# Where VectorE's share of the low parts stands, and which buffer holds their h: a fused attention and maxout kernel

## The chip, the core and the metric

One core of a Trainium2 chip. TensorE multiplies matrices (in the profile PE, with PEld for its weight loads), VectorE (DVE), ScalarE (ACT) and GpSimd (POOL) work on elements, SyncE's queue (SP) starts DMAs. SBUF is the working memory, PSUM holds eight banks of 128 x 512 f32 that TensorE writes. The metric is the time on the device in microseconds (us) of one execution. Before the change it is 818.93 us, the median of three runs from 818.26 to 819.09.

## The reference

```python
def _attn_ref(x, inducing):                    # x: (4, 12544, 128), inducing: (32, 128)
    def mab(q, kv):
        s = scale * (q @ kv.transpose(0, 2, 1))
        s = s - s.max(-1, keepdims=True)
        a = np.exp(s)
        a /= a.sum(-1, keepdims=True) + 1e-09
        return a @ kv
    h = mab(I, x)
    return mab(x, h).astype(np.float32)

def _moe_ref(x, w1, w2, w3, w_out):            # w1, w2, w3: (128, 768), w_out: (768, 128)
    h = np.maximum(np.maximum(x @ w1, x @ w2), x @ w3)
    return (h @ w_out).astype(np.float32)
```

The output of the first goes through the second, all in f32.

## The kernel before, in words

For each of the four batches, a first phase pools all tokens into 32 states h (softmax over tokens), and a second phase computes, for every token, softmax weights over those 32 states and from them the maxout and the last product. The first phase of batch 0 runs alone at the start; from then on the second phase of one batch runs with the first phase of the next beside it.

**The second phase's pipeline.** The 98 tiles of 128 tokens of a batch are one short group of 2 tiles and six full groups of 16. A full group is four chunks of 512 columns, and each chunk has six slots, one for each 128 of the 768 hidden units. So a full group is a window of 24 slots, numbered 0 to 23 here, and is called by (batch, group). For each slot:

- TensorE multiplies the weights `pT` with two sets of columns into the banks `pu` (line 819) and `pv` (825), which alternate between two banks each;
- ScalarE takes the relu of `pu` (834), VectorE the maximum of that and `pv` (852): this is `h`, 128 x 512;
- ScalarE rounds `h` to fp32r, the high part `hi` (841), and one engine subtracts that from `h`, the low part `lo`: GpSimd (849) for most slots, VectorE (855) for a few;
- six slots later TensorE adds wo_hi x hi, wo_lo x hi and wo_hi x lo to the chunk's output bank `acc` (898). At the first of a chunk's slots a product of its own (894) starts that bank afresh.

There are two output banks (`bank_o`). While one collects a chunk, the other holds the chunk before until it is copied out (`finish`, 910), and is idle after that until the next chunk's line 894; `spare[0]` names it.

**What sets the order.** `main` writes the instructions of all engines slot by slot, by hand, and each engine runs its own in that order. `advance` writes a slot: a subtraction that VectorE is to do is kept in `pipe["low"]` and written one step after GpSimd's would be, behind the maximum of the slot two on. Beside the slots, `plan` puts other work at chosen slots of a window:

- `softmax2`: the weights of the next group, VectorE and ScalarE steps at slots 3 to 15 (742 to 776);
- `turn`: the first phase of the next batch, 18 turns in all, one a window from (0,1) to (2,4). TensorE writes scores at slot 2, which holds up the slots' products for about 3 us; VectorE reduces them at slot 4 (407); GpSimd swaps the maxima between partition halves and quarters by small copies L429 at slots 5 and 9 (`turn_swap`; a copy L419 at slot 4 adds the last maximum); VectorE reduces the swapped ones by L437 at slots 8 (`mq`) and 11 (`mm`). Windows (0,1) and (0,2) have a second turn 12 slots later, whose last products come at slot 14 of the window after;
- in group 5 the next batch's states are put together (`invert_total`, `combine_states`, `combine_low`).

**Which slots are VectorE's.** `Chunk.low` says for which slots VectorE subtracts; `in_bank` says whether the `h` of such a slot is written to the second `aux` bank (`bank_a[1]`) or to one of five SBUF buffers `h`. Which slots the bank is free for follows from `first_free`. Before the change that is, for batches 0 to 2: slots 4, 15, 18, 21 in groups 1 to 4 (slot 4 in SBUF, the others in the bank), but 4, 16, 18, 21 in group 5 and in (0,1) and (0,2), all in SBUF, and 4, 16, 18, 21 in group 6, the last two in the bank. The last batch has slots 0, 5, 14, 18, 21, all in the bank. In all 36 subtractions have both operands in SBUF and 66 one in a bank.

Of the kernel before, what the change touches and what calls it, by code (L numbers as in the profile page):

```python
# [8 lines left out]
F32 = mybir.dt.float32  # L9
# [16 lines left out]
def kernel(ctx, tc, x, xt, ind_t, w1, w2, w3, w_out, out):  # L26
    nc = tc.nc
    B, N, C = x.shape
    M = ind_t.shape[1]
    DF = w1.shape[1]  # L30
    P = 128
    NT = N // P
    NJ = DF // P
# [4 lines left out]
    OB = 2  # L38
# [16 lines left out]
    ORDER = "a a b a a b a b 0 w l a b a a b b 1 2 a b p c b P s X 3 Y S z s s s s s b s"  # L55
    STEPS2 = (3, 6, 7, 8, 9, 10, 11, 12, 14, 15)
    scale = 1.0 / float(C) ** 0.5
    LOWVEC = (4, 16, 18, 21)
    LOWBANK = (4, 15, 18, 21)
    LOWLAST = (0, 5, 14, 18, 21)  # L60
    OUTVEC = (0, 2)
    UW = 2 * DF + C
# [3 lines left out]
    groups = []  # L66
    t0 = 0
    while t0 < NT:
        nt = NT % GT if t0 == 0 and NT % GT else GT
# [4 lines left out]
    NG = len(groups)  # L74
# [5 lines left out]
    const = ctx.enter_context(tc.tile_pool(name="const", bufs=1))  # L80
    wk = ctx.enter_context(tc.tile_pool(name="wk", bufs=2))
    bp = ctx.enter_context(tc.tile_pool(name="bp", bufs=2))
    hp = ctx.enter_context(tc.tile_pool(name="hp"))
# [3 lines left out]
    bank_a, bank_u, bank_v, bank_o = (  # L87
        [ps.tile([P, 512], F32, name=f"{n}{i}", tag=f"{n}{i}") for i in range(2)] for n in ("aux", "pu", "pv", "acc")
    )

    spare = [None]
# [26 lines left out]
    xts_free = [const.tile([P, GT * P], F32, name=f"xT{i}", tag=f"xT{i}") for i in range(XTB)]  # L118
    xgs_free = [const.tile([P, GT, C], F32, name=f"xg{i}", tag=f"xg{i}") for i in range(XB)]
    w_space = xts_free.pop()  # L120
    shelf = const.tile([P, UW + 2 * groups[0]["nt"] * P + 2 * P + 2 * M + OB * 512 + groups[0]["nt"] * C], F32, name="shelf")
    shelf_at = [0]

    def place(n):
        shelf_at[0] += n
        return shelf[:, shelf_at[0] - n : shelf_at[0]]
# [2 lines left out]
    short_t = [place(groups[0]["nt"] * P) for i in range(2)]  # L129
    short_x = place(groups[0]["nt"] * C).rearrange("p (t c) -> p t c", c=C)  # L130
    iT = place(M)

    def load_raw(src):
        r = bp.tile([P, 2 * DF], U32, name="raw", tag="raw", bufs=4)
        shape = r if len(src.shape) == 2 else r.rearrange("p (j c) -> p j c", j=NJ)
        nc.sync.dma_start(out=shape, in_=src)
        return r
# [43 lines left out]
    def convert(k):  # L181

        v = raws[k].rearrange("p (k two) -> p two k", two=2)
        low, high = v[:, 0, :], v[:, 1, :]

        def temp(dt, name):
# [63 lines left out]
    def start_batch(b):  # L250
        st = state[b] = {"xT": {}, "xg": {}, "a": {}, "s": {}}
        if b == 0:
            st["lst"] = bp.tile([P, NG], F32, name="lst", tag="lst", bufs=1)
            st["mneg"] = bp.tile([P, NG], F32, name="mneg", tag="mneg", bufs=1)
            st["hg"] = outs[1].rearrange("p (g c) -> p g c", c=C)
        else:
            st["mm"] = bp.tile([P, NK], F32, name="mm", tag="mm")
            st["fac"] = bp.tile([P, NK], F32, name="fac", tag="fac")
            st["hs"] = bp.tile([P, C + 1], F32, name="hs", tag="hs")

    def load_tokens(b, k):
        for gi in turns[k]:
# [248 lines left out]
    def phase1_first():  # L511

        start_batch(0)
        nc.sync.dma_start(out=iT, in_=ind_t)
        nc.scalar.mul(out=iT, in_=iT, mul=scale)
# [36 lines left out]
        for step in STEPS1.split():  # L552
# [5 lines left out]
            else:  # L558
                groupwise[step[0]](int(step[1:]))
        xts_free.append(w_space)  # L560
        start_batch(1)
        load_channels(1, 0)

# [248 lines left out]
    def advance():  # L812

        s = pipe["next"]
        pipe["next"] += 1
        if s + 1 < len(slots):
            c, j = slots[s + 1]
            pu, w = bank_u[(s + 1) % 2], c.w
            nc.tensor.matmul(  # L819
                out=pu[:, :w], lhsT=state[c.b]["us"][:, 2 * j * P : (2 * j + 1) * P], rhs=c.pT[:, :w], start=True, stop=True  # L820
            )
        if 0 <= s < len(slots):
            d, j = slots[s]
            pv = bank_v[s % 2]
            nc.tensor.matmul(  # L825
                out=pv[:, : d.w],
                lhsT=state[d.b]["us"][:, (2 * j + 1) * P : (2 * j + 2) * P],
                rhs=d.pT[:, : d.w],
                start=True,
                stop=True,  # L830
            )
        if s + 1 < len(slots):
            ru = hp.tile([P, 512], F32, name="ru", tag="ru", bufs=3)
            nc.scalar.activation(out=ru[:, :w], in_=pu[:, :w], func=AF.Relu)  # L834
            relus[s + 1] = ru
        low = pipe.pop("low", None)
        if 0 <= s - 1 < len(slots):
            c, j = slots[s - 1]
            h = sums.pop(s - 1)
            hi = hp.tile([P, 512], F32R, name="hi", tag="hi", bufs=9)  # L840
            nc.scalar.copy(out=hi[:, : c.w], in_=h[:, : c.w])  # L841
            lo = hp.tile([P, 512], F32R, name="lo", tag="lo", bufs=10)
            c.hh.append(hi)
            c.hl.append(lo)
            args = dict(out=lo[:, : c.w], in0=h[:, : c.w], in1=hi.bitcast(F32)[:, : c.w])
            if c.low(j):
                pipe["low"] = args
            else:
                nc.gpsimd.tensor_sub(**args)  # L849
        if 0 <= s < len(slots):  # L850
            h = bank_a[1] if d.in_bank(slots[s][1]) else hp.tile([P, 512], F32, name="h", tag="h", bufs=5)
            nc.vector.tensor_max(out=h[:, : d.w], in0=pv[:, : d.w], in1=relus.pop(s)[:, : d.w])  # L852
            sums[s] = h
        if low:
            nc.vector.tensor_sub(**low)  # L855

    class Chunk:
# [8 lines left out]
                self.key = "B" if q else "A"  # L866
                self.base = 0 if q is None else groups[0]["nt"] if q == 0 else (q - 1) * TC

        def low(self, k):

            if self.q is None:
                return False
            if self.b + 1 == B:
                return NJ * self.q + k in LOWLAST
            return NJ * self.q + k in (LOWVEC if self.first_free() > min(LOWBANK[1:]) else LOWBANK)

        def first_free(self):

            if self.b + 1 == B:
                return 0  # L880
            if self.gi == NG - 2 or self.b == 0 and self.gi < 3:
                return WIN
            return 18 if self.gi == NG - 1 else 13

        def in_bank(self, k):

            return self.low(k) and NJ * self.q + k >= self.first_free()

    def stage2(c, j):
        us = state[c.b]["us"]  # L890
# [54 lines left out]
    slots = [(c, j) for c in chunks for j in range(NJ)]  # L945
# [3 lines left out]
    WIN = NQ * NJ  # L949
# [39 lines left out]
    for i in range(B * NW):  # L989
        b, g = i // NW, i % NW + 1  # L990
# [9 lines left out]
    for n in range(1, B):  # L1000
# [16 lines left out]
        st = ("state", n)  # L1017
# [16 lines left out]
    def main():  # L1034
        over = None
        for s in range(len(slots) + LAG + 1):

            if s >= LAG:
                spare[0] = bank_o[((s - LAG) // NJ + 1) % 2]
            if pipe["next"] <= s:  # L1040
                advance()
            k = s // NJ + AHEAD
            if s % NJ == 4 and k < len(chunks) and k > NQ:
                chunks[k].pT = probs(chunks[k])
            if s // NJ < NQ and s % NJ == (0, 1, 2, 2)[s // NJ] and s >= NJ:
                chunks[s // NJ + 1].pT = probs(chunks[s // NJ + 1])
            if over:
                (finish if over.n + 1 < len(chunks) else finish_last)(over)
                over = None
            if s == len(slots) + LAG:  # L1050
                break
            for f, args in plan[s]:
                f(*[state[a[1]] if isinstance(a, tuple) and a[0] == "state" else a for a in args])
            if s >= LAG:
                c, j = slots[s - LAG]
                stage2(c, j)
                if j == NJ - 1:
                    over = c

    with tc.manual_schedule(engines=MANUAL):  # L1060
        phase1_first()
        st = state[0]
# [5 lines left out]
        for step in ORDER.split():  # L1068
            if step == "p":
                chunks[0].pT = probs(chunks[0], bank_u[0])  # L1070
            elif step == "P":
                chunks[1].pT = probs(chunks[1], bank_u[1])
            elif step == "c":
                nc.scalar.copy(out=wcat[:, 2 * DF :], in_=bank_u[1][:, :C])
                first_products(st, 3, bank_o[0])
            elif step == "l":
                nc.gpsimd.tensor_sub(out=wo_lo, in0=wo, in1=wo_hi.bitcast(F32))
            elif step == "s":
                advance()
            elif step == "S":  # L1080
                scores_products(0, 2, bank_a[0])
            elif step in steps:
                next(steps[step])
            elif step[0] == "F":
                unread_products(int(step[1:]), bank_v[0][:, 2 * P :])
            elif step in "0123":
                first_high(st, int(step))
            elif step in "wxyz":
                first_low(st, "wxyz".index(step), nc.gpsimd)
            else:  # L1090
                first_low(st, "WXYZ".index(step), nc.vector)
# [59 lines left out]
```

## Time and profile before

| | before |
|---|---|
| median of the runs shown | 818.93 us |
| the profiled execution's own time | 818.5 us |
| its span, first to last instruction | 816.7 us |
| granted TensorE clock | 1.000 |
| PE busy | 806.1 us, 4565 instructions |
| DVE busy | 654.7 us, 1198 instructions |
| ACT busy | 719.2 us, 1446 instructions |
| POOL busy | 661.1 us, 640 instructions |

Rows of a timeline give the start in us from the span's start, the duration in us, the engine, the line, the operation and what it writes and reads; in brackets stands idle time of the engine just before it and what ended that. A merged row (x4) has the first start and the time to the last end. Rows of waits give who waited for whom: us in total, times, the longest. Rows by tile give the least, the median and the greatest duration in ns, and the first and last start in us. VectorE starts its next instruction some 0.08 us before the one ahead of it ends, so a 0.68 us instruction takes 0.60 us of its time. The durations of matmuls are of pipelined ones: their starts count.

### The profile page before, as it was taken

Reading aid. Unit: us, or ns where it says so; the run is one execution under the profiler, and the core shown is the slowest. Engines: PE = TensorE matmul, PEld = TensorE weight load, DVE = VectorE, ACT = ScalarE, POOL = GpSimd, SP = SyncE. Lnnn points to the kernel's source line nnn. Section 1 sums busy time; section 2 is a strip of 40 time slices with the busy share of each in tenths; the row PEclk is TensorE's granted clock in tenths of the full one; section 3 lists DMA queues with packets and bytes.
Section 4 is the critical chain, followed back from the end, with each engine's and each line's share of the span. In section 5 each row is a group of like instructions: output and inputs, shape, how many; then the busy total and the mean of one; then the engine's idle time right before and its main releaser. Section 6 shows DMA issues by size and latency. Waiting matters only on the chain.

```text
span 816.7 us, 15025 instructions
## 1 busy us (share of the span) xinstructions
PE 806.1 (99%) x4565; PEld 628.3 (77%) x4565; DVE 654.7 (80%) x1198; ACT 719.2 (88%) x1446; POOL 661.1 (81%) x640
## 2 busy tenths in 40 slices
PE   8999999999999999999999999999999999999998
PEld 5667778777787787777777777877778778777886
DVE  6889778787796797887987978878789878878874
ACT  6779889898898898988988989989889999999996
POOL 0369898798798987977988889889878888878886
PEclk9999999999999999999999999999999999999999
DMA  9334643543553335335453353344232222222221
GB/s 344 140 149 141 212 148 106 183 125 105 157 173 123 126 112 175 125 106 177 130 159 117 110 175 120 110 127 126 59 98 66 84 65 78 69 81 74 62 79 51
DMA packets 45408, 101.47 MB, mean 124 GB/s; under 512 B 9360, under 2 KB 15376, under 8 KB 40208
## 3 DMA queue, kind: packets, MB, share of 16 engines
q1 hardware_dynamic: 45184, 100.39, 38.6%
q8 instruction: 36, 0.59, 0.3%
q14 instruction: 44, 0.36, 0.1%
q10 hardware_dynamic: 144, 0.13, 0.0%
HBM read 48.12 MB, written 25.69 MB: 90 GB/s over the span
## 4 chain that ended last, share of the span: by engine, by line
PE 92%; DVE 3%; DMA 2%; ACT 1%; issue 1%; POOL 0%; SPq 0%; DVEq 0%; ACTq 0%
PE acc L898 49%; PE pv L825 16%; PE pu L819 16%; PE aux L707 3%; PE acc L894 3%; PE acc L485 2%; PE aux L388 2%; DMA raw<-in_w_dram 2%; DMA xg<-in_x_dram 1%; POOL rest L207 0%; DVE h L852 0%; ACT ru L834 0%; PE aux L669 0%; DVE mx L745 0%; ACT hi L841 0%
## 5 line engine op out<-in xcount | busy, mean ns | idle before, releaser
L849 POOL TENSOR_TENSOR lo<-h,hi 128x512 fp32r<-128x512 f32 (+1 forms) x498 | 626.6, 1288 | 107.3 <-ACT hi L841 61.8
L852 DVE TENSOR_TENSOR h<-pv,ru 128x512 f32<-128x512 f32 (+1 forms) x534 | 356.2, 672 | 129.6 <-PE pv L825 100.7
L834 ACT ACTIVATE ru<-pu 128x512 f32<-128x512 f32 (+1 forms) x600 | 367.6, 613 | 66.5 <-PE pu L819 62.1
L841 ACT CAST hi<-h 128x512 fp32r<-128x512 f32 (+1 forms) x534 | 333.5, 625 | 4.7 <-DVE h L852 3.6
L898 PE MATMUL acc<-hi,wo_hi 128*128 128x512 f32 (+1 forms) x601 | 235.0, 391 | 0.0
L825 PE MATMUL pv<-pT,us 128*128 128x512 f32 (+1 forms) x600 | 232.7, 388 | 1.6 <-DVE h L852 1.4
L819 PE MATMUL pu<-pT,us 128*128 128x512 f32 (+1 forms) x600 | 231.9, 387 | 0.1
L898 PE MATMUL acc<-hi,wo_lo 128*128 128x512 f32 (+1 forms) x601 | 231.5, 385 | 0.0
L898 PE MATMUL acc<-lo,wo_hi 128*128 128x512 f32 (+1 forms) x601 | 231.3, 385 | 0.0
L898 PEld LDWEIGHTS acc<-hi,wo_hi 128*128 128x128 f32 x601 | 112.8, 188 | 41.5 <-issue 20.5
L825 PEld LDWEIGHTS pv<-pT,us 128*128 128x128 f32 x600 | 112.6, 188 | 29.3 <-DVE h L852 5.4
L819 PEld LDWEIGHTS pu<-pT,us 128*128 128x128 f32 x600 | 112.6, 188 | 24.6 <-ACT ru L834 1.7
L898 PEld LDWEIGHTS acc<-lo,wo_hi 128*128 128x128 f32 x601 | 112.8, 188 | 23.0
L898 PEld LDWEIGHTS acc<-hi,wo_lo 128*128 128x128 f32 x601 | 112.9, 188 | 21.8
L852 DVE TENSOR_TENSOR aux<-pv,ru 128x512 f32<-128x512 f32 x66 | 45.9, 695 | 11.8 <-PE pv L825 5.3
L855 DVE TENSOR_TENSOR lo<-aux,hi 128x512 fp32r<-128x512 f32 x66 | 45.2, 686 | 0.8 <-PE acc L898 0.8
L841 ACT CAST hi<-aux 128x512 fp32r<-128x512 f32 x66 | 41.3, 626 | 0.1
L910 ACT COPY shelf<-acc 128x512 f32<-128x512 f32 (+1 forms) x65 | 39.3, 604 | 0.0
L894 PE MATMUL acc<-pT,us 128*128 128x512 f32 (+1 forms) x100 | 38.8, 388 | 0.0
L855 DVE TENSOR_TENSOR lo<-h,hi 128x512 fp32r<-128x512 f32 x36 | 30.0, 833 | 0.4 <-PE acc L898 0.2
L207 POOL TENSOR_TENSOR rest<-rest,t 128x768 f32<-128x768 f32 x2 | 3.7, 1828 | 28.7 <-DVE rest L203 23.6
L429 POOL COPY mq<-mq 32x1 f32<-32x1 f32 (+2 forms) x108 | 20.4, 188 | 5.2
(166 smaller groups left out, 545.9 us busy)
## 6 DMA issues: line engine op xcount, KB each, us to landing
out_dram<-shelf SPq DMA_DIRECT2D x95, 256.0 KB, 2.0
xg<-in_x_dram SPq DMA_DIRECT2D x22, 1024.0 KB, 5.7
xT<-in_xt_dram SPq DMA_DIRECT2D x18, 1024.0 KB, 5.0
pT<-ph SPq DMA_DIRECT2D x184, 64.0 KB, 2.0
pT<-pl SPq DMA_DIRECT2D x184, 64.0 KB, 2.0
raw<-in_w_dram SPq DMA_DIRECT2D x3, 768.0 KB, 15.0
us<-uh SPq DMA_DIRECT2D x24, 52.0 KB, 2.7
us<-ul SPq DMA_DIRECT2D x24, 52.0 KB, 1.9
```

The lines of the kernel that those rows point to most:

```text
L429: nc.gpsimd.tensor_copy(out=far[to : to + step], in_=own[lo : lo + step])
L707: nc.tensor.matmul(out=sp[q * M : (q + 1) * M, :w], lhsT=st["hT"][:, :M], rhs=xT[:, q * w : (q + 1) * w], start=True, stop=True)
L819: nc.tensor.matmul(out=pu[:, :w], lhsT=state[c.b]["us"][:, 2 * j * P : (2 * j + 1) * P], rhs=c.pT[:, :w], start=True, stop=True)
L825: nc.tensor.matmul(out=pv[:, : d.w], lhsT=state[d.b]["us"][:, (2 * j + 1) * P : (2 * j + 2) * P], rhs=d.pT[:, : d.w], start=True, stop=True,)
L834: nc.scalar.activation(out=ru[:, :w], in_=pu[:, :w], func=AF.Relu)
L841: nc.scalar.copy(out=hi[:, : c.w], in_=h[:, : c.w])
L849: nc.gpsimd.tensor_sub(**args)
L852: nc.vector.tensor_max(out=h[:, : d.w], in0=pv[:, : d.w], in1=relus.pop(s)[:, : d.w])
L855: nc.vector.tensor_sub(**low)
L894: nc.tensor.matmul(out=c.acc[:, :w], lhsT=us[:, 2 * DF :], rhs=c.pT[:, :w], start=True, stop=False)
L898: nc.tensor.matmul(out=c.acc[:, cs], lhsT=lhs[:, j, :], rhs=rhs[j][:, cs], start=False, stop=(j == NJ - 1 and rhs is c.hl and cs.stop == w),)
L910: (nc.vector.tensor_copy if by_vector else nc.scalar.copy)(out=o[:, : c.w], in_=c.acc[:, : c.w])
```

## The change

The rules `low`, `first_free` and `in_bank` give way to one table, which says for each window which slots are VectorE's and where their `h` lies: "a" is the `aux` bank as before, "o" the idle output bank, "h" an SBUF buffer. For batches 0 to 2:

| window | before | after |
|---|---|---|
| groups 1 to 4, but (0,1) and (0,2) | 4 h, 15 a, 18 a, 21 a | 15 a, 18 a, 20 o, 21 a |
| (0,1) | 4, 16, 18, 21 h | 4 h, 16 h, 20 o |
| (0,2) | 4, 16, 18, 21 h | 4 h, 8 o, 20 o |
| group 5 | 4, 16, 18, 21 h | 8 o, 14 o, 20 o |
| group 6 | 4 h, 16 h, 18 a, 21 a | 14 o, 18 a, 20 o, 21 a |

The last batch is as before. VectorE has 97 subtractions in place of 102 (3 in SBUF, 28 in the output bank, 66 in the `aux` bank), GpSimd five more. The sums `hs` of a turn, two buffers, move from a pool to two places on the `shelf` tile. The lines behind the table have other numbers in the changed kernel: its 443 is 437 before, 425 is 419, 435 is 429, 855 is 849, 861 is 852, 864 is 855, 890 is 894, 906 is 910.

```diff
-    LOWVEC = (4, 16, 18, 21)
-    LOWBANK = (4, 15, 18, 21)
+    LOWS = {15: "a", 18: "a", 20: "o", 21: "a"}
+    LOWS_AT = {
+        (0, 1): {4: "h", 16: "h", 20: "o"},
+        (0, 2): {4: "h", 8: "o", 20: "o"},
+        **{(b, 5): {8: "o", 14: "o", 20: "o"} for b in range(3)},
+        **{(b, 6): {14: "o", 18: "a", 20: "o", 21: "a"} for b in range(3)},
+    }
...
+    sums_at = [place(C + 1) for _ in range(2)]
...
-            st["hs"] = bp.tile([P, C + 1], F32, name="hs", tag="hs")
+            st["hs"] = sums_at[b % 2]
...
-            if c.low(j):
+            if c.home(j):
                 pipe["low"] = args
             else:
                 nc.gpsimd.tensor_sub(**args)
         if 0 <= s < len(slots):
-            h = bank_a[1] if d.in_bank(slots[s][1]) else hp.tile([P, 512], F32, name="h", tag="h", bufs=5)
+            home = d.home(slots[s][1])
+            h = {"a": bank_a[1], "o": spare[0]}.get(home)
+            if h is None:
+                h = hp.tile([P, 512], F32, name="h", tag="h", bufs=5)
...
-        def low(self, k):
+        def home(self, k):
...
+            lows = dict.fromkeys(LOWLAST, "a") if self.b + 1 == B else LOWS_AT.get((self.b, self.gi), LOWS)
+            return lows.get(NJ * self.q + k)
```

On GpSimd, around the turn of window (1,1), the order before is this: the first row holds the subtractions of slots 0 to 3, then the copy of the last maximum, the first swap, the subtractions of slots 5 to 8, and the second swap.

```order
L849 TENSOR_TENSOR lo<-h,hi 128x512 x4
L419 COPY mq<-mm 128x1
L429 COPY mq<-mq 64x1 x2
L849 TENSOR_TENSOR lo<-h,hi 128x512 x4
L429 COPY mq<-mq 32x1 x4
```

And in the changed kernel, at the same place:

```order
L855 TENSOR_TENSOR lo<-h,hi 128x512 x4
L425 COPY mq<-mm 128x1
L855 TENSOR_TENSOR lo<-h,hi 128x512
L435 COPY mq<-mq 64x1 x2
L855 TENSOR_TENSOR lo<-h,hi 128x512 x4
L435 COPY mq<-mq 32x1 x4
```

The subtraction of slot 4 has come to GpSimd, between the copy of the last maximum and the first swap; the second swap has five subtractions ahead of it behind that copy, where it had four.

On VectorE, in window (1,5) from the maximum of slot 9 to that of slot 13, before (`pv_75` and `pv_74` are the two `pv` banks, `aux_70` and `aux_71` the `aux` banks, `acc_76` and `acc_77` the output banks):

```order
L852 TENSOR_TENSOR h<-pv_75,ru 128x512
L753 TENSOR_REDUCE aux_71<-aux_70 128x16
L852 TENSOR_TENSOR h<-pv_74,ru 128x512
L755 TENSOR_SCALAR aux_71<-aux_71 128x16
L852 TENSOR_TENSOR h<-pv_75,ru 128x512
L757 RECIPROCAL rs<-aux_71 128x16
L758 TENSOR_TENSOR aux_70<-aux_70,rs 128x512
L437 TENSOR_REDUCE mm<-mq 128x1
L852 TENSOR_TENSOR h<-pv_74,ru 128x512
L910 COPY shelf<-acc_76 128x512
L770 STREAM_TRANSPOSE aux_70<-aux_70 128x512
L852 TENSOR_TENSOR h<-pv_75,ru 128x512
```

In the changed kernel, from the same maximum on:

```order
L861 TENSOR_TENSOR h<-pv_75,ru 128x512
L759 TENSOR_REDUCE aux_71<-aux_70 128x16
L861 TENSOR_TENSOR h<-pv_74,ru 128x512
L864 TENSOR_TENSOR lo<-acc_77,hi 128x512
L761 TENSOR_SCALAR aux_71<-aux_71 128x16
L861 TENSOR_TENSOR h<-pv_75,ru 128x512
L763 RECIPROCAL rs<-aux_71 128x16
L764 TENSOR_TENSOR aux_70<-aux_70,rs 128x512
L443 TENSOR_REDUCE mm<-mq 128x1
L861 TENSOR_TENSOR h<-pv_74,ru 128x512
L906 COPY shelf<-acc_76 128x512
L776 STREAM_TRANSPOSE aux_70<-aux_70 128x512
```

The subtraction of slot 8, with its `h` in the output bank `acc_77`, stands behind the maximum of slot 10; nothing else has moved there.

More of the change, by code (lines that the diff above doesn't have):

```diff
@@ L120 @@
     w_space = xts_free.pop()
-    shelf = const.tile([P, UW + 2 * groups[0]["nt"] * P + 2 * P + 2 * M + OB * 512 + groups[0]["nt"] * C], F32, name="shelf")
+    shelf = const.tile([P, UW + 2 * groups[0]["nt"] * P + 2 * P + 2 * M + OB * 512 + groups[0]["nt"] * C + 2 * (C + 1)], F32, name="shelf")
     shelf_at = [0]
@@ L867, in __init__ @@
                 self.base = 0 if q is None else groups[0]["nt"] if q == 0 else (q - 1) * TC
-        def low(self, k):
+        def home(self, k):
             if self.q is None:
[L872 to L887, printed above, removed]
+                return None
+            lows = dict.fromkeys(LOWLAST, "a") if self.b + 1 == B else LOWS_AT.get((self.b, self.gi), LOWS)
+            return lows.get(NJ * self.q + k)
     def stage2(c, j):
```

## The prediction

> **What bounds the kernel now.** I read the chain of work that ended last first, then who waited for whom on TensorE (PE), then the order of time around each wait. A window is called (batch, group), and a slot by its place 0 to 23 in it; us throughout.
>
> ```profile
> PE 92%; DVE 3%; DMA 2%; ACT 1%; issue 1%; POOL 0%; SPq 0%; DVEq 0%; ACTq 0%
> ```
> ```profile
> PEld pv L825 <- DVE h L852: 5.0, 11, 1.2
> DVE h L852 <- PE pv L825: 100.7, 121, 3.6
> ```
>
> The chain is TensorE nearly everywhere, so only its waits and its added work count. Past the first 60 us the one wait that VectorE causes it is `pv` for the maximum two slots earlier, which still reads that `pv` bank: 5.0 us at most (the weight load's idle time, a little more than the matmul's), in 11 places. The other way round VectorE stands idle 100.7 us for TensorE, in 121 places over the whole span: it has room in general, and none in a few stretches. Most of that time has the following look, in window (1,4):
>
> ```profile
> 353.67 2.98 POOL L849 TENSOR_TENSOR lo<-h,hi 128x512 fp32r<-128x512 f32 x2 [0.35 <-PE acc L898]
> 353.72 1.79 DVE L855 TENSOR_TENSOR lo<-h,hi 128x512 fp32r<-128x512 f32 x1
> ...
> 356.04 0.68 DVE L852 TENSOR_TENSOR h<-pv,ru 128x512 f32<-128x512 f32 x1
> ...
> 355.63 0.39 PE L819 MATMUL pu<-pT,us 128*128 128x512 f32 x1
> 356.77 0.50 PE L825 MATMUL pv<-pT,us 128*128 128x512 f32 x1 [0.74 <-DVE h L852]
> ```
> ```profile
> L855 DVE TENSOR_TENSOR lo<-aux,hi x66: 673/687/693, 142.0 to 809.0; 128x512 fp32r<-128x512 f32 x66
> L855 DVE TENSOR_TENSOR lo<-h,hi x36: 665/681/1828, 61.5 to 624.6; 128x512 fp32r<-128x512 f32 x36
> ```
>
> VectorE's low part of slot 4, both operands in SBUF, starts 0.05 behind a subtraction of GpSimd (POOL) and takes 1.79 in place of the median 0.681; with the other operand in a bank none of 66 took over 0.693. The maximum comes late, and `pv` starts 0.73 behind that maximum's start and 1.14 behind `pu`. Ordinary pitch here is 0.23 (300.39 to 300.63 below), so TensorE lost 0.91, and its first matmul after the wait lasts 0.50 where others last 0.39: 1.02 in all. The same happens twice in (2,6):
>
> ```profile
> 611.15 0.39 PE L819 MATMUL pu<-pT,us 128*128 128x512 f32 x1
> 612.23 0.50 PE L825 MATMUL pv<-pT,us 128*128 128x512 f32 x1 [0.70 <-DVE h L852]
> ...
> 626.55 0.39 PE L819 MATMUL pu<-pT,us 128*128 128x512 f32 x1
> 627.03 0.50 PE L825 MATMUL pv<-pT,us 128*128 128x512 f32 x1
> ```
>
> That is (1.08 - 0.23 + 0.11) + (0.48 - 0.23 + 0.11) = 1.32.
>
> **The change, part by part.**
>
> *Low parts leave SBUF.* Of 36 such subtractions 3 stay, 28 go to the idle output bank, 5 more in all go to POOL. The waits just shown go: -1.02 and -1.32. A bank costs nothing by the rows (0.687 against 0.681). [...]
>
> *Slot 4 becomes POOL's.* This is the term that decides. On POOL the new subtraction stands between the copy L419 and the two copies L429 that swap the maxima of the next batch's turn, ahead of four more subtractions and the four copies L429 of the second swap. VectorE's L437 (`mm`) waits for those. Window (1,2) before:
>
> ```profile
> 290.40 0.20 POOL L419 COPY mq<-mm 128x1 f32<-128x1 f32 x1
> 290.66 0.40 POOL L429 COPY mq<-mq 64x1 f32<-64x1 f32 x2
> 291.44 5.27 POOL L849 TENSOR_TENSOR lo<-h,hi 128x512 fp32r<-128x512 f32 x4 [0.38 <-ACT hi L841]
> 296.77 0.83 POOL L429 COPY mq<-mq 32x1 f32<-32x1 f32 x4
> 297.68 6.33 POOL L849 TENSOR_TENSOR lo<-h,hi 128x512 fp32r<-128x512 f32 x5
> ...
> 289.53 0.61 ACT L841 CAST hi<-h 128x512 fp32r<-128x512 f32 x1
> ```
> ```profile
> 297.88 0.15 DVE L437 TENSOR_REDUCE mm<-mq 128x1 f32<-128x3 f32 x1
> 297.95 0.68 DVE L852 TENSOR_TENSOR h<-pv,ru 128x512 f32<-128x512 f32 x1
> 298.54 0.68 DVE L910 COPY shelf<-acc 128x512 f32<-128x512 f32 x1
> 299.14 0.72 DVE L770 STREAM_TRANSPOSE aux<-aux 128x512 f32<-128x512 f32 x1
> 299.77 0.66 DVE L852 TENSOR_TENSOR h<-pv,ru 128x512 f32<-128x512 f32 x1
> ...
> 300.63 0.39 PE L825 MATMUL pv<-pT,us 128*128 128x512 f32 x1
> ```
>
> The swap ends at 297.60 and L437 begins at 297.88: 0.28 to spare. Now add the subtraction. `hi` of slot 4 is there at 290.14, L419 ends at 290.60. Subtraction 290.66 to 291.96 (1.30; five in 6.33 are a pitch of 1.26); two copies 292.02 to 292.42; four subtractions 292.50 to 297.57 (3 x 1.26 + 1.30, the first no longer held up by VectorE's); four copies 297.63 to 298.46; L437 at 298.49, which is 0.61 later. VectorE has no room behind it: the rows down to the maximum of slot 13 follow each other at 0.60, so that comes at 300.38, and `pv` of slot 15 can start 0.73 after it, at 301.11 in place of 300.63. TensorE waits 0.48, plus the 0.11 of the next matmul: +0.59.
>
> That L437 does stop VectorE, and 0.03 behind the copies, this row of before shows:
>
> ```profile
> 116.39 1.37 POOL L429 COPY mq<-mq 32x1 f32<-32x1 f32 x4
> ...
> 117.79 0.16 DVE L437 TENSOR_REDUCE mm<-mq 128x1 f32<-128x3 f32 x1 [0.51 <-POOL mq L429]
> ```
>
> From the end of L419 to that `pv` is 10.03 in (1,2), and by the same sum 10.51 after. First and last of the eight windows alike, (0,4) and (2,4):
>
> ```profile
> 159.42 0.20 POOL L419 COPY mq<-mm 128x1 f32<-128x1 f32 x1
> 169.63 0.39 PE L825 MATMUL pv<-pT,us 128*128 128x512 f32 x1
> ...
> 546.98 0.20 POOL L419 COPY mq<-mm 128x1 f32<-128x1 f32 x1
> 557.20 0.39 PE L825 MATMUL pv<-pT,us 128*128 128x512 f32 x1
> ```
>
> 10.01 and 10.02. Eight windows, (0,4), (0,6), (1,2), (1,3), (1,6), (2,2), (2,3), (2,4): 8 x 0.59 = +4.7. Window (1,4) is the ninth, +0.59 beside its -1.02. In (0,3) TensorE has products of a turn at slot 14 that give VectorE time: nothing. In (1,1), and alike in (2,1), the chunk is behind the short one and POOL is further back:
>
> ```profile
> 259.68 0.17 POOL L419 COPY mq<-mm 128x1 f32<-128x1 f32 x1
> 266.75 0.16 DVE L437 TENSOR_REDUCE mm<-mq 128x1 f32<-128x3 f32 x1
> 268.67 0.67 DVE L852 TENSOR_TENSOR h<-pv,ru 128x512 f32<-128x512 f32 x1
> 269.39 0.50 PE L825 MATMUL pv<-pT,us 128*128 128x512 f32 x1
> ```
>
> 259.85 + 10.51, and 0.03 for the longer stretch 266.75 to 268.67, is 270.39, against 269.39, where TensorE had waited already: +1.00 each, the small waits that slot 4 cost there being counted in it.
>
> *Slot 8 in group 5.* Subtraction 8 comes behind the maximum of slot 10, where VectorE has 0.3 to spare but not 0.6. In (1,5):
>
> ```profile
> 391.08 0.17 DVE L755 TENSOR_SCALAR aux<-aux 128x16 f32<-128x16 f32 x1
> 391.42 0.69 DVE L852 TENSOR_TENSOR h<-pv,ru 128x512 f32<-128x512 f32 x1 [0.17 <-ACT hi L841]
> 394.81 0.67 DVE L852 TENSOR_TENSOR h<-pv,ru 128x512 f32<-128x512 f32 x1
> ...
> 395.66 0.40 PE L825 MATMUL pv<-pT,us 128*128 128x512 f32 x1
> ```
>
> L755 moves from 391.08 to 391.68, the next maximum to 391.76 (+0.34), that of slot 13 to 395.15, `pv` of slot 15 to 395.88: 0.22 and 0.11. Three such windows, the last with a little more room: +0.9. POOL is no cause here: with slot 8 gone its second swap comes a subtraction earlier.
>
> *Costed at nothing.* Slots 14 and 20 in the bank: their subtraction, issued two slots on, falls where VectorE mostly waits for `pv` anyhow (part of the 100.7), and the L894 that overwrites the bank comes four slots on, two slots of TensorE's time after it. Now L894 waits for that subtraction, and behind it on TensorE stands everything. No row of before shows such a wait. Its price lies between 0 and the 0.60 of one more VectorE instruction, at each of 28 places; I take 0, nearest to a VectorE that is waiting itself, and keep half of the other end for a rival. Slots 16, 18 and 21 where they go to POOL: POOL has just skipped a slot or is about to, and L898 wants the result only six slots after the maximum. `hs` on the shelf: two buffers as before, nothing.
>
> **Sum.** -1.02 - 1.32 + 4.7 + 0.59 + 2.0 + 0.9 = +5.9 on the profiled execution's span of 816.7, and so 824.4 for its own time of 818.5; the median of the runs shown, 818.93, is 0.4 above that, well within what is uncertain. Predicted: 824.4.
>
> **Rivals.** *POOL keeps up, and the change is faster.* If the second swap ended by 298.0 in (1,2), L437 would lose at most the 0.12 that slot 13 has to spare, and no new wait arises: -2.3, and about -1 (an estimate, from what is left of the 5.0) for the small old waits of (1,1) and (2,1), against +0.9 of slot 8: 2.4 less, 816.1. That needs POOL half a us faster over the five subtractions and six copies, about 1.16 a subtraction in place of 1.26. For it: POOL's rows beside VectorE's SBUF subtractions are lengthened (2.98 for two, above), and those go. Against it: the five at 1.26 run with none beside them. [...] I give it 0.10.
>
> *Half of it.* The new waits are there but less than half as long, because POOL's hand-overs at the copies (0.06 and 0.08 a time as I add them) or the subtraction itself are shorter: 9 x 0.25 + 2 x 0.66 + 0.9 - 2.3 = +2.1, 820.6, or by some 2 about it. I give it 0.12.
>
> *Worse: the bank is a new wait.* L894, which waited for nobody, waits for the subtraction in its bank. If the late VectorE of the turn windows is still late at slots 20 to 23, each costs some 0.3 more: 28 x 0.3 = 8, 832. Against it: the 100.7 us in which VectorE waits for TensorE. I give it 0.05.
>
> **How the numbers follow.** Forecast 0.73, by itself 821.5 to 827 (waits of 0.35 to 0.75 in the eight windows). The range 819 to 827 adds most of the halved case. About 0.2% (1.6 us) is what a measurement of this kernel can tell from no change: faster 0.10, the same 0.08, slower 0.82.
>
> **What would show it.** Right: L437 (`mm`) idle for POOL's L429 in ten or more windows; `pv` of slot 15 waiting some 0.5 for the maximum there, at 10.5 from the end of L419's counterpart; no VectorE `lo` over 0.7 in the bank. Wrong: L437 never idle, or POOL's subtractions near 1.1. Slot 8: `pv` of slot 15 in group 5 waiting 0.2. The bank: L894 never waiting for VectorE.

## The result, and the profile after

| kernel | median us (range, runs) | span of the profiled execution, us |
|---|---|---|
| before | 818.89 (818.26 to 819.09, 4) | 816.7 |
| after | 823.12 (823.0 to 823.8, 4) | 821.2 |

The change makes the kernel slower: 1.0055 times the time of before, 95% interval 1.0037 to 1.0072, or 4.2 us. In the line numbers of after, L825 is the `pu` product (L819 before), L831 `pv` (L825), L861 the maximum (L852), L864 VectorE's low part (L855), L855 POOL's (L849), L425, L435 and L443 the copy of the last maximum, the copies of the swaps and `mm` (L419, L429 and L437), L890 and L894 the products into the output bank (L894 and L898).

The chain of work that ended last, by engine, in the changed kernel:

```profile
PE 81%; DVE 6%; POOL 3%; ACT 3%; issue 3%; DMA 2%; SPq 0%; POOLq 0%; DVEq 0%
```

TensorE holds 81% of it where it held 92%. VectorE and POOL have three points more each, POOL from 0%, and ScalarE (ACT) and the time in which nothing was waited for (issue) two each. The waits between 60 and 700 us show where the engines come in. The columns are the total in us, the number of places, the longest one:

```profile
PEld pv L831 <- DVE h L861: 10.1, 15, 0.9
...
DVE mm L443 <- POOL mq L435: 6.7, 12, 1.3
...
PE pv L831 <- DVE h L861: 3.8, 13, 0.5
```

The weight loads' idle time ahead of `pv` has doubled from 5.0 us (the first row; the last row is the matmuls' own), and one step back on the path stands what causes it: `mm`, which waited 0.5 us for POOL in one place before, waits 6.7 us in twelve. Reading one of the twelve, window (1,2), by the order of time gives the whole path, POOL's rows first:

```profile
292.35 0.19 POOL L425 COPY mq<-mm 128x1 f32<-128x1 f32 x1
292.49 1.30 POOL L855 TENSOR_TENSOR lo<-h,hi 128x512 fp32r<-128x512 f32 x1
293.85 0.40 POOL L435 COPY mq<-mq 64x1 f32<-64x1 f32 x2
294.33 5.06 POOL L855 TENSOR_TENSOR lo<-h,hi 128x512 fp32r<-128x512 f32 x4
299.45 0.83 POOL L435 COPY mq<-mq 32x1 f32<-32x1 f32 x4
```
```profile
299.22 0.70 DVE L764 TENSOR_TENSOR aux<-aux,rs 128x512 f32<-128x512 f32 x1
300.32 0.16 DVE L443 TENSOR_REDUCE mm<-mq 128x1 f32<-128x3 f32 x1 [0.40 <-POOL mq L435]
...
302.23 0.67 DVE L861 TENSOR_TENSOR h<-pv,ru 128x512 f32<-128x512 f32 x1
...
302.34 0.39 PE L825 MATMUL pu<-pT,us 128*128 128x512 f32 x1
302.95 0.50 PE L831 MATMUL pv<-pT,us 128*128 128x512 f32 x1 [0.22 <-DVE h L861]
```

The subtraction at 292.49 is slot 4's, new on POOL. Five subtractions, two copies of the first swap and four of the second later, the second swap ends at 300.28. VectorE has been done with L764 since 299.92 and stands idle; `mm` starts 0.04 behind the copies, the maximum of slot 13 comes at 302.23, and `pv` of slot 15 starts 0.61 behind `pu` where 0.23 is the ordinary pitch. TensorE loses 0.38, and 0.11 more because this matmul lasts 0.50 in place of 0.39. In (2,4), the last of the windows alike, the same two rows stand just as far apart:

```profile
562.17 0.39 PE L825 MATMUL pu<-pT,us 128*128 128x512 f32 x1
562.78 0.50 PE L831 MATMUL pv<-pT,us 128*128 128x512 f32 x1 [0.22 <-DVE h L861]
```

What the change removes has gone as well. The durations of VectorE's low parts (min/median/max in ns) by where their h is, `acc` being the idle output bank:

```profile
L864 DVE TENSOR_TENSOR lo<-aux,hi x66: 671/691/693, 141.5 to 813.5; 128x512 fp32r<-128x512 f32 x66
L864 DVE TENSOR_TENSOR lo<-acc,hi x28: 675/681/693, 81.1 to 633.9; 128x512 fp32r<-128x512 f32 x28
L864 DVE TENSOR_TENSOR lo<-h,hi x3: 681/684/684, 60.8 to 94.0; 128x512 fp32r<-128x512 f32 x3
```

None is longer than 0.693 us; before, the longest took 1.828.

### The profile page after: what moved, and what is told of

It is laid out like the page before. It is cut to its first block, busy times and chain, and to the rows that moved or that the text cites. A ratio compares the mean times of both kernels' runs of the same rounds, so it can differ in the third digit from the quotient of the medians.

```text
span 821.2 us, 15006 instructions
## 1 busy us (share of the span) xinstructions
PE 808.2 (98%) x4565; PEld 628.6 (77%) x4565; DVE 649.7 (79%) x1193; ACT 721.3 (88%) x1446; POOL 657.7 (80%) x645
## 4 chain that ended last, share of the span: by engine, by line
PE 81%; DVE 6%; POOL 3%; ACT 3%; issue 3%; DMA 2%; SPq 0%; POOLq 0%; DVEq 0%
PE acc L894 43%; PE pv L831 14%; PE pu L825 14%; PE aux L713 3%; POOL lo L855 2%; DMA xg<-in_x_dram 2%; DVE h L861 2%; PE acc L890 2%; PE aux L394 2%; PE acc L491 2%; DVE shelf L906 1%; ACT hi L847 1%; ACT ru L840 1%; POOL mq L435 1%; DVE aux L776 1%
## 5 line engine op out<-in xcount | busy, mean ns | idle before, releaser
L855 POOL TENSOR_TENSOR lo<-h,hi 128x512 fp32r<-128x512 f32 (+1 forms) x503 | 625.0, 1273 | 115.8 <-ACT hi L847 57.7
L861 DVE TENSOR_TENSOR h<-pv,ru 128x512 f32<-128x512 f32 (+1 forms) x506 | 338.2, 672 | 129.3 <-PE pv L831 99.1
L847 ACT CAST hi<-h 128x512 fp32r<-128x512 f32 (+1 forms) x506 | 313.4, 619 | 2.1 <-DVE h L861 0.9
L831 PE MATMUL pv<-pT,us 128*128 128x512 f32 (+1 forms) x600 | 233.5, 389 | 3.9 <-DVE h L861 3.8
L894 PE MATMUL acc<-hi,wo_hi 128*128 128x512 f32 (+1 forms) x601 | 235.0, 391 | 0.0
L825 PE MATMUL pu<-pT,us 128*128 128x512 f32 (+1 forms) x600 | 231.8, 386 | 0.1
L894 PE MATMUL acc<-hi,wo_lo 128*128 128x512 f32 (+1 forms) x601 | 231.5, 385 | 0.0
L894 PE MATMUL acc<-lo,wo_hi 128*128 128x512 f32 (+1 forms) x601 | 231.4, 385 | 0.0
L894 PEld LDWEIGHTS acc<-hi,wo_hi 128*128 128x128 f32 x601 | 112.8, 188 | 41.8 <-issue 20.5
L831 PEld LDWEIGHTS pv<-pT,us 128*128 128x128 f32 x600 | 112.6, 188 | 33.4 <-DVE h L861 10.4
L825 PEld LDWEIGHTS pu<-pT,us 128*128 128x128 f32 x600 | 112.6, 188 | 24.7 <-ACT ru L840 1.7
L894 PEld LDWEIGHTS acc<-lo,wo_hi 128*128 128x128 f32 x601 | 112.8, 188 | 23.0
L894 PEld LDWEIGHTS acc<-hi,wo_lo 128*128 128x128 f32 x601 | 112.9, 188 | 21.8
L861 DVE TENSOR_TENSOR aux<-pv,ru 128x512 f32<-128x512 f32 x66 | 45.9, 695 | 10.0 <-PE pv L831 4.0
L864 DVE TENSOR_TENSOR lo<-aux,hi 128x512 fp32r<-128x512 f32 x66 | 45.3, 686 | 0.3 <-PE pv L831 0.3
L890 PE MATMUL acc<-pT,us 128*128 128x512 f32 (+1 forms) x100 | 38.9, 389 | 0.0
L861 DVE TENSOR_TENSOR acc<-pv,ru 128x512 f32<-128x512 f32 x28 | 19.4, 694 | 7.0 <-PE pv L831 5.4
L713 PE MATMUL aux<-xT,hT 128*32 128x512 f32 x184 | 24.5, 605 | 0.0
```

Of the source, the lines that this page charges most:

```text
L713: nc.tensor.matmul(out=sp[q * M : (q + 1) * M, :w], lhsT=st["hT"][:, :M], rhs=xT[:, q * w : (q + 1) * w], start=True, stop=True)
L825: nc.tensor.matmul(out=pu[:, :w], lhsT=state[c.b]["us"][:, 2 * j * P : (2 * j + 1) * P], rhs=c.pT[:, :w], start=True, stop=True)
L831: nc.tensor.matmul(out=pv[:, : d.w], lhsT=state[d.b]["us"][:, (2 * j + 1) * P : (2 * j + 2) * P], rhs=d.pT[:, : d.w], start=True, stop=True,)
L890: nc.tensor.matmul(out=c.acc[:, :w], lhsT=us[:, 2 * DF :], rhs=c.pT[:, :w], start=True, stop=False)
L894: nc.tensor.matmul(out=c.acc[:, cs], lhsT=lhs[:, j, :], rhs=rhs[j][:, cs], start=False, stop=(j == NJ - 1 and rhs is c.hl and cs.stop == w),)
```

## The experiments

**Swap theory**: POOL's subtraction of slot 4 stands ahead of the four copies of the second swap, and their lateness passes through `mm` and a maximum to `pv` of slot 15. **Bank theory**: the new work at slot 20 and its bank is what costs. **Load theory**: POOL as a whole has too much. Times are medians, each with its ratio to the kernel before (818.6 to 818.8 us in these runs) and the 95% interval.

### Two undo runs: slot 4 alone, slot 20 alone

`e1_slot4_back`: slot 4 goes back to VectorE, slot 20 stays.

```diff
-LOWS = {15: "a", 18: "a", 20: "o", 21: "a"}
+LOWS = {4: "h", 15: "a", 18: "a", 20: "o", 21: "a"}
-    **{(b, 6): {14: "o", ...
+    **{(b, 6): {4: "h", 14: "o", ...
```

> Slot 4 is given back to VectorE, in SBUF, in the ordinary windows and in group 6 (13 windows); slot 20 stays with VectorE in the output bank. Swap theory (POOL's subtraction of slot 4 stands ahead of the four copies of the second swap, VectorE's `mm` comes late, and with it the maximum of slot 13 and `pv` of slot 15): L443 never idle for L435 for more than 0.1 us in these windows; the nine waits of 0.50 us and the 1.9 us more in (1,1) and (2,1) go, 6.4 us in all: 823.1 - 6.4 = 816.7 us, and up to 2.3 us more where VectorE's subtraction of slot 4 is again lengthened to 1.8 us as in the kernel before: 816.5 to 819.8 us. Bank theory (the new work of slot 20 and its bank is what costs): the bank is used as before this edit, so 823 us or above, since VectorE has 13 subtractions more.

Measured: 817.99 us, 0.9993 (0.9984 to 1.0002). No wait of `mm` for POOL is left past 60 us, and the waits of `pv` have fallen from 10.1 us in 15 places to this:

```profile
PEld pv L831 <- DVE h L861: 3.4, 8, 1.1
```
```profile
L864 DVE TENSOR_TENSOR lo<-h,hi x16: 666/681/1828, 61.0 to 609.0; 128x512 fp32r<-128x512 f32 x16
```

The second row has one lengthened subtraction again, at 609.0 us, and TensorE waits 0.85 us behind it: the old loss, in one place of the three.

`e2_no_slot20`: slot 20 is taken away, slot 4 stays with POOL.

```diff
-LOWS = {15: "a", 18: "a", 20: "o", 21: "a"}
+LOWS = {15: "a", 18: "a", 21: "a"}
-    **{(b, 6): {14: "o", 18: "a", 20: "o", 21: "a"} ...
+    **{(b, 6): {14: "o", 18: "a", 21: "a"} ...
```

> Slot 20 is taken from VectorE in the same 13 windows and goes to POOL; slot 4 stays with POOL, as in the changed kernel. Swap theory: what stands ahead of the second swap is the same, so `pv` of slot 15 waits in the same windows by the same 0.50 us; only the one L890 wait of 0.15 us may go: 822.5 to 823.5 us. Bank theory: 13 of the 28 subtractions in the bank go, and with them half the loss or more: 818.9 to 821 us. Load theory (POOL as a whole has too many subtractions): 13 subtractions of 1.26 us more on POOL, so slower, 824 us or above, with L894 waiting for POOL's `lo`.

Measured: 823.43 us, 1.0059 (1.0046 to 1.0072), the time of the changed kernel.

```profile
PEld pv L831 <- DVE h L861: 9.9, 14, 0.9
DVE mm L443 <- POOL mq L435: 7.0, 12, 1.4
```

Both waits are as in the changed kernel. 13 subtractions fewer on VectorE and in the bank win nothing, and 13 more on POOL, behind the swap, cost nothing: against the bank theory and against the load theory.

### Slot 4 alone, put into the kernel before

`e8_before_slot4_pool`:

```diff
-return NJ * self.q + k in (LOWVEC if self.first_free() > min(LOWBANK[1:]) else LOWBANK)
+return NJ * self.q + k in (LOWVEC if self.first_free() == WIN else LOWVEC[1:] if self.first_free() == 18 else LOWBANK[1:])
```

> The kernel before, with one edit: slot 4 goes to POOL in the 13 ordinary and group 6 windows; no bank, no slot 20, nothing else of the change. Swap theory: this alone makes the loss. Nine waits of 0.50 us and 1.9 us more in (1,1) and (2,1) come, and the 2.3 us of waits behind the lengthened SBUF subtractions go: 818.8 + 6.4 - 2.3 = 822.9 us, 822 to 823.6. Bank theory: without the bank only the gain is left, 818.8 - 2.3 = 816.5 us. Load theory: POOL has 13 subtractions more than before, against 5 more in the changed kernel, so above 823.6 us.

Measured: 823.19 us, 1.0057 (1.0043 to 1.0071). With the line numbers of before:

```profile
PEld pv L825 <- DVE h L852: 9.2, 13, 0.9
DVE mm L437 <- POOL mq L429: 7.3, 13, 1.3
```

Slot 4 given to POOL makes the loss by itself, with no slot in the output bank, and `pv` of slot 15 waits 0.39 to 0.41 us in the nine windows.

### The swap moved, with no work moved between engines

`e4_swap_early` is the changed kernel with one number changed:

```diff
-at(s + 7, turn_swap, b, k, M)
+at(s + 6, turn_swap, b, k, M)
```

> The changed kernel with nothing moved between the engines: only the four copies of the second swap are issued one slot earlier on POOL, ahead of the subtraction of slot 8. Swap theory: in (1,2) the copies end near 299.0 in place of 300.28 us, which is before VectorE is done with L764 (299.92), so L443 never waits for L435, and the waits of `pv` of slot 15 (nine of 0.50 us, and 1.9 us more in (1,1) and (2,1)) go: 823.1 - 6.4 = 816.7 us, 816 to 818, and so faster than both kernels; the 0.2 us waits of group 5 stay. Bank theory and load theory: the subtractions, banks and POOL's sum are the same, so 823 us. Against the swap theory from inside: the copies wait for VectorE's first L443 and hold up POOL, and the L894 then wait for `lo`: 819 us or above.

Measured: 816.05 us (815.72 to 816.1), 0.9967 (0.9954 to 0.9979): faster than both kernels. Window (1,2), POOL and then VectorE:

```profile
292.25 3.81 POOL L855 TENSOR_TENSOR lo<-h,hi 128x512 fp32r<-128x512 f32 x3
296.12 0.84 POOL L435 COPY mq<-mq 32x1 f32<-32x1 f32 x4
297.04 5.07 POOL L855 TENSOR_TENSOR lo<-h,hi 128x512 fp32r<-128x512 f32 x4
```
```profile
297.12 0.70 DVE L764 TENSOR_TENSOR aux<-aux,rs 128x512 f32<-128x512 f32 x1
297.72 0.15 DVE L443 TENSOR_REDUCE mm<-mq 128x1 f32<-128x3 f32 x1
```
```profile
PEld pv L831 <- DVE h L861: 1.0, 3, 0.4
```

Three subtractions and not four stand ahead of the swap, it ends at 296.96, and `mm` follows L764 with nothing between. The waits of `pv` shrink from 10.1 to 1.0 us. What POOL does, and how much of it, is unchanged; only its order is.

`e9_before_swap_late` is the opposite dose, on the kernel before (`s + 7` becomes `s + 8`).

> The kernel before, with the four copies of the second swap issued one slot later on POOL, behind one more subtraction; which engine does what is untouched. Swap theory, as a dose: in (1,2) the copies end 1.26 us later, near 298.9, L443's counterpart L437 is 1.01 later, the maximum of slot 13 0.60 x 3 behind that, and `pv` of slot 15 waits 0.9 us and the next matmul 0.11, twice what the change did: nine windows times 1.0 and some 1.3 each in (1,1) and (2,1), 818.8 + 9 + 2.6 = 830.4 us, 828 to 832. Bank theory and load theory: nothing they speak of is changed, so 818.8 us.

Measured: 834.38 us, 1.0194 (1.018 to 1.0208): the direction and the mechanism, but 4 us above the forecast and outside its range. Window (1,2):

```profile
305.72 0.16 DVE L437 TENSOR_REDUCE mm<-mq 128x1 f32<-128x3 f32 x1 [0.92 <-POOL mq L429]
...
306.09 0.39 PE L819 MATMUL pu<-pT,us 128*128 128x512 f32 x1
306.55 0.50 PE L825 MATMUL pv<-pT,us 128*128 128x512 f32 x1
307.58 0.40 PE L819 MATMUL pu<-pT,us 128*128 128x512 f32 x1
308.36 0.50 PE L825 MATMUL pv<-pT,us 128*128 128x512 f32 x1 [0.38 <-DVE h L852]
```

Here `pv` of slot 14 waits too: 0.46 - 0.23 + 0.11 = 0.34, then 0.78 - 0.23 + 0.11 = 0.66 at slot 15, together the 1.0 expected. The miss is in the count. Five windows that I had not reckoned with, (0,1), (0,2), (0,3), (0,5) and (1,5), have no room for 1.26 us either: they are longer than before by 0.41, 1.09, 0.67, 0.95 and 0.95 us, 4.1 between them, and 830.4 + 4.1 = 834.5. `mm` waits in 18 places, against 12 in the changed kernel:

```profile
DVE mm L437 <- POOL mq L429: 18.2, 18, 1.5
```

`e6_before_swap_early` is the control: the kernel before with `s + 6`.

> The control for the early swap: the kernel before, with the second swap's four copies one slot earlier and nothing else. Swap theory: before the change L437 came by its own engine's order with 0.28 us to spare in (1,2), so nothing is won there; only the small waits of (1,1) and (2,1), 0.4 us in all, can go: 818.0 to 818.9 us, with the waits behind the lengthened SBUF subtractions in about the same number (they hang on how POOL's and VectorE's starts meet, and may move by 1 us). If the early swap is good by itself, by some way that has nothing to do with slot 4: 816.5 us or less.

Measured: 816.27 us, 0.9971 (0.9959 to 0.9982). I was wrong: the early swap helps the kernel before as well, by 2.4 us, though `mm` had waited for POOL in one place only, for 0.5 us.

```profile
L855 DVE TENSOR_TENSOR lo<-h,hi x36: 664/681/1682, 61.2 to 621.8; 128x512 fp32r<-128x512 f32 x36
...
PEld pv L825 <- DVE h L852: 1.5, 4, 0.5
```

The trace says by which way. The lengthened subtractions that cost TensorE 1.02 us in (1,4) and 1.32 in (2,6) are ordinary ones now, and 2.34 of the 2.4 us are these. In (1,4) the two starts have changed places:

```profile
352.64 0.68 DVE L855 TENSOR_TENSOR lo<-h,hi 128x512 fp32r<-128x512 f32 x1
352.95 4.04 POOL L849 TENSOR_TENSOR lo<-h,hi 128x512 fp32r<-128x512 f32 x3 [0.34 <-PE acc L898]
```

VectorE is 0.31 us ahead of POOL, where before it was 0.05 behind, and now POOL's three take 4.04 where three take 3.81 in the rows of `e4_swap_early`; the last section shows that this order of the starts decides which of the two is lengthened. Why the starts shift so is not settled; the early copies change POOL's phase in all windows. It means that `e4_swap_early` gets under the kernel before by no merit of the change: 816.05 and 816.27 are the same within the intervals. What `e4_swap_early` does show is 7.1 us between it and the changed kernel from the order alone.

### Slot 8

`e3_slot8`: in the ten ordinary windows VectorE takes slot 8 in place of slot 20.

```diff
-LOWS = {15: "a", 18: "a", 20: "o", 21: "a"}
+LOWS = {8: "o", 15: "a", 18: "a", 21: "a"}
```

> In the ten ordinary windows VectorE takes slot 8 in the output bank in place of slot 20; slot 4 stays with POOL. So one subtraction fewer stands ahead of the second swap on POOL, as in the kernel before, but VectorE has its 0.60 us at slot 10, ahead of the same `mm`. Swap theory: L443 does not wait for L435 any more; VectorE had 0.32 and 0.40 us of idle time there in (1,2), so that about 0.2 us of the 0.60 are left over at the maximum of slot 13 and `pv` of slot 15 waits 0.2 to 0.3 us in place of 0.5, some 0.3 us less in eight windows of the nine and 0.3 to 0.6 less in (1,1) and (2,1): 823.1 - 3 = 820 us, 819 to 821. Bank theory: as many banks and subtractions as before the edit, so 823 us.

Measured: 818.98 us, 1.0004 (0.9996 to 1.0013), 0.02 us under the range. One subtraction less ahead of the swap takes away most of what the early swap does: `mm` waits for POOL in two places and not in twelve. The price on VectorE is less than I reckoned: `pv` of slot 15 waits 0.05 to 0.07 us in the ordinary windows, not 0.2 to 0.3. (0,6) and (1,6), which the edit leaves alone, keep their 0.42 to 0.43: a control within the same run.

`e5_swap_early_no8`: `e4_swap_early` with slot 8 of group 5 back on POOL.

```diff
-**{(b, 5): {8: "o", 14: "o", 20: "o"} for b in range(3)},
+**{(b, 5): {14: "o", 20: "o"} for b in range(3)},
```

> The changed kernel with the early second swap, and in group 5 slot 8 goes back to POOL (three windows). By the prediction's step on slot 8: the waits of `pv` of slot 15 there, 0.23, 0.23 and 0.10 us with 0.11 behind each, go: 816.05 - 0.9 = 815.2 us. If slot 8 is not their cause, or POOL is then late with something else in that window: 816 us or more.

Measured: 815.60 us, 0.9964 (0.9951 to 0.9976). By time it can't be told from `e4_swap_early`. The trace can tell: the three windows of group 5 are 0.35, 0.34 and 0.25 us shorter than in `e4_swap_early`, 0.9 in all. In (1,5) `pv` of slot 15 follows `pu` at the ordinary pitch, where it was 0.46 behind in the changed kernel (397.83 and 398.29):

```profile
394.62 0.39 PE L825 MATMUL pu<-pT,us 128*128 128x512 f32 x1
394.85 0.39 PE L831 MATMUL pv<-pT,us 128*128 128x512 f32 x1
```

### What the bank is worth

`e7_all_sbuf` and `e10_all_sbuf_early` put the h of all 28 bank slots into SBUF (every `"o"` of the table becomes `"h"`), the one with the swap as in the changed kernel, the other with the early swap.

> The changed kernel with the h of all its 28 bank slots (8, 14 and 20) in SBUF; which engine does what, and in which order, stays. If an SBUF home is what lengthens VectorE's subtraction (five of 36 took 1.68 to 1.83 us in the kernel before, none of 28 in a bank took over 0.693): between one and ten of the 28 take more than 1 us, each costs TensorE 0 to 1.0 us, and the waits for the second swap stay: 823 to 828 us, 824.5 by the share of the kernel before. If the lengthening belonged to slot 4's place and not to SBUF: none over 0.7 us and 823.1 us. Bank theory: the bank's waits go, so below 822 us.

> The same with the second swap one slot earlier, so that no wait for it covers the bank's worth: against 816.05 us with the bank. If SBUF lengthens: some subtractions over 1 us, 816 to 821 us. If the bank is worth nothing in this kernel: 816 us. Bank theory: below 815.5 us.

Measured: 823.98 us, 1.0065 (1.0051 to 1.0078), and 817.59 us, 0.9988 (0.9979 to 0.9997). VectorE's low parts with h in SBUF in the two:

```profile
L864 DVE TENSOR_TENSOR lo<-h,hi x31: 679/683/1308, 61.3 to 634.7; 128x512 fp32r<-128x512 f32 x31
```
```profile
L864 DVE TENSOR_TENSOR lo<-h,hi x31: 680/682/1849, 61.5 to 628.8; 128x512 fp32r<-128x512 f32 x31
```

In the first, two of 31 are over 1 us (1.31 and 1.29), and TensorE waits 0.13 and 0.12 us for them; in the second four are (1.85 twice, 1.15, 1.14), none of them at slot 4, and the longest two cost 0.67 and 0.65 us. Behind each of these waits comes 0.11 more. The first of these, in (0,6), with POOL's row for the time around it:

```profile
237.22 1.85 DVE L864 TENSOR_TENSOR lo<-h,hi 128x512 fp32r<-128x512 f32 x1
...
235.97 5.48 POOL L855 TENSOR_TENSOR lo<-h,hi 128x512 fp32r<-128x512 f32 x4
...
239.16 0.39 PE L825 MATMUL pu<-pT,us 128*128 128x512 f32 x1
240.06 0.50 PE L831 MATMUL pv<-pT,us 128*128 128x512 f32 x1 [0.51 <-DVE h L861]
```

So with an SBUF home the subtraction can be lengthened at other slots than 4 too (the last section shows when), and in the bank none was. It is worth about 1.5 us with the early swap (817.59 against 816.05); in the changed kernel's order the 0.9 us between the medians is little beside their scatter, and the two waits with what is behind them are 0.47 us of it.

## Why the prediction was right, and where its sizes were off

Forecast 824.4 us, range 819 to 827; measured 823.12. The likeliest case is the one that happened. By its terms, in us of TensorE's time. What was found is how much longer a window became, from the start of its first `pv` to that of the next window's; the waits in the cells are times from one start to the next beyond the usual pitch:

| term | predicted | found in the trace of after |
|---|---|---|
| waits in (1,4) and (2,6) gone | -2.34 | -1.1 and -1.5: -2.6 |
| eight windows and (1,4): `pv` of slot 15 | 9 x 0.59 = 5.3 | 9 waits of 0.38 to 0.42, 0.11 behind each: 4.6 |
| (1,1) and (2,1) | 2.0 | 0.9 each: 1.8 |
| slot 8 in group 5 | 0.9 | 0.35, 0.35 and 0.19: 0.9 |
| slot 8 in (0,2) | not counted | 0.2 |
| bank, `hs`, slots 16, 18, 21 | 0 | one wait of L890: 0.2 |
| sum | +5.9 | +5.1 |

Two things that the prediction did not see cancel, by luck, and so do not show in the sum: the low parts that left SBUF won 2.60 us and not 2.34, and the new slot 8 of (0,2), which the table of the change lists beside those of group 5, costs 0.24. There VectorE runs without a gap from that subtraction (98.81) to the sum of the turn, L462 at 103.46, and TensorE's next scores wait for it:

```profile
103.70 1.06 PE L394 MATMUL aux<-xT,shelf 128*32 128x512 f32 x8 [0.25 <-DVE shelf L462]
```

In all eight profiles of kernels with that slot 8 on VectorE the window is 0.24 to 0.29 us longer than before. No run takes it back alone, so this cause is read from the rows and not tested. The prediction took `pv` for TensorE's one wait for VectorE past 60 us; the same view of before has six smaller ones, 2.3 us in all, and this place is among them, with 0.2.

**Slot 4 becomes POOL's: the mechanism holds.** `e8_before_slot4_pool` has the loss with this step alone, `e1_slot4_back` loses it by taking the step back, `e4_swap_early` by taking away only its place ahead of the copies, and `e9_before_swap_late` makes it larger with the place alone. The size was off by one hand-over. I let the subtraction start 0.06 us behind the end of L425; it starts at 292.49, and L425 ends at 292.54, so 0.11 us were given away in each window. From there on the sum fits: the copies end at 300.28, `mm` follows by 0.04 and `pv` of slot 15 by 2.63 more, where I had 2.62. It took 10.41 us from the end of L425 to that `pv`, and not 10.51.

(1,1), where TensorE had waited already, shows the same chain with two `pv` behind it, those of slots 14 and 15. I had forecast its sum and not that it falls into two:

```profile
268.70 0.16 DVE L443 TENSOR_REDUCE mm<-mq 128x1 f32<-128x3 f32 x1 [1.32 <-POOL mq L435]
...
269.52 0.50 PE L831 MATMUL pv<-pT,us 128*128 128x512 f32 x1 [0.47 <-DVE h L861]
271.33 0.50 PE L831 MATMUL pv<-pT,us 128*128 128x512 f32 x1 [0.38 <-DVE h L861]
```

**The start.** The table's 5.1 us is more than the spans differ by (4.5). The first `pu` of the main loop comes earlier in the profile of after than in that of before:

```profile
47.21 0.36 PE L825 MATMUL pu<-pT,us 128*128 128x256 f32 x1
```
```profile
47.86 0.36 PE L819 MATMUL pu<-pT,us 128*128 128x256 f32 x1
```

That is 0.65, and 4.5 + 0.65 = 5.15. In the twelve profiles of this study this first `pu` starts anywhere between 47.2 and 48.1 us, in kernels that do the same work up to there, so I take the 0.65 as scatter of the start.

**The rivals.** *POOL keeps up* failed where it was expected to fail: four subtractions on POOL take 5.06 us, a pitch of 1.26, where it needed about 1.16. The gain that it counted on did come: VectorE's lengthened subtractions went, none with one operand in a bank took over 0.693 us in the changed kernel, and in the last two experiments four and six of 31 with both in SBUF took 0.83 to 1.85 us, each of them beside one of POOL's. But that gain is the worth of an instruction's neighbours, not of what queues behind it. *Half of it* was nearer in its reason than in its size: a hand-over was indeed shorter, by 0.11 and not by 0.34. *The bank is a new wait* came true in one place, 0.04 us of waiting and 0.11 behind it, at the edge of (0,6):

```profile
244.57 0.68 DVE L864 TENSOR_TENSOR lo<-acc,hi 128x512 fp32r<-128x512 f32 x1
...
245.31 0.50 PE L890 MATMUL acc<-pT,us 128*128 128x512 f32 x1
```

The subtraction ends at 245.25 and the product that overwrites the bank starts at 245.31. No other place of the 28 shows such a wait. The bank's own duration was taken rightly from the rows of before: medians of 0.681 us in the bank and of 0.681 to 0.684 in SBUF.

**Costed at nothing.** `e8_before_slot4_pool` has neither the output bank, nor `hs` on the shelf, nor the other slots given to POOL. That its median, 823.19, is that of the changed kernel shows nothing yet, since it lacks the slots 8 and their loss too, and its five runs scatter from 822.04 to 823.49. The windows of the two profiles tell more: they are equal within 0.05 us, but for (0,2), (1,5) and (2,5), where the changed kernel has its slot 8, and (1,0), where the wait of L890 falls; these four are 1.2 us longer in it. (In (0,5) both lose 0.35, the one by slot 8, the other by a maximum that starts 0.3 late for a reason that was not followed up.) So what was costed at nothing is worth nothing together, but for that one wait; `hs` was not tried alone.

## What to carry to other kernels

When an instruction is given to another engine, read what stands behind it in that engine's queue before adding up loads: here one subtraction of 1.26 us, on an engine with time to spare (POOL was busy for 657.7 of 821.2 us), delayed four tiny copies (0.83 us together), and the engine that waited for them passed the delay on to TensorE. Where a small step is waited for and a large one is not, give the small one its place first; one number in the order was worth 7.1 us, with no work moved. And apply such a cure to the kernel before as well: without that control I would have credited the change with a gain that the old kernel gets from the same edit.

## What the runs showed that was not expected

How often VectorE's subtraction with both operands in SBUF is lengthened does not go by how many there are. With the same 36 of them, the kernel before has five over 1 us, the early swap three, behind which TensorE nowhere waits over 0.2 us, and the late swap two. It goes by which engine starts first, and not only in (1,4), where VectorE's took 1.79 us with POOL 0.05 us ahead and 0.68 with VectorE 0.31 us ahead. The twelve profiles together hold 224 such subtractions. Of these, 195 start while POOL is not subtracting and take 0.66 to 0.70 us. The other 29 start inside one of POOL's subtractions, and 25 of them end 0.55 to 0.59 us after POOL's has ended, which makes them 0.68 to 1.83 us long; in the last four, one of POOL's starts lies within 0.02 us of VectorE's, and there either engine may be the one that is lengthened. POOL pays in its turn: in the kernel before, its subtractions that start inside one of VectorE's ordinary ones take 1.44 to 1.69 us, where 1.30 is usual. With one operand in a bank VectorE's take 0.67 to 0.70 us in all 384 places where POOL is subtracting as they start. So an edit that only shifts one engine's phase moved this kernel by 2.4 us, though the step that it moved was waited for in one place only.
